# Attention and a gated feed-forward layer on one core: output tiles staged in reused load buffers, an exp and a mask emitted earlier, a weight fusion begun one step later

## The chip, the cores and the metric

One core of one Trainium2 chip. The metric is the device time of one execution in microseconds (us), lower is better. Executions of one kernel here spread by more than 1% to either side (the kernel before: 320.1 to 328.0 us in 34 runs of the first group, up to 330.1 us in another), so medians and many runs are used. With one core there is no second die to compare; a run counts as slow here only because it lies over 1.5% above the fastest of its kernel in the group. Two single executions lie far from all others and are unexplained: one of 1622 us among 35 runs of the kernel before (their median is 324.68 us with it and 324.50 without) and one of 1011 us in `only_buffers` (left out).

## The reference

```python
# attention: B=8, H=8, S=576, D=64, 16 extra "beacon" keys seen by every query
k_all  = concat([beacon_k, k]); v_all = concat([beacon_v, v])
scores = scale * q @ k_all.T           # causal on the 576 keys
a      = softmax(scores); x = a @ v_all  # -> 4608 tokens x 512
# feed-forward: d_model 512, d_ff 1024
h   = ((x @ w1) * (x @ w2)) @ w3
out = h @ w_out                        # 4608 x 512, float32
```

## The kernel before

The kernel fuses `w3 @ w_out` once into one 1024x512 matrix `Wt`, so the feed-forward layer is two products, a multiply and one more product. Attention runs in 64 steps (a pair of heads, half of the query tiles). Each step emits: the scores of the next step (TensorE), two exps of them (ScalarE), one or two masks (VectorE), the value matmuls of this step (TensorE), and between them "fill": a slice of the feed-forward matmuls of an earlier token chunk, drawn one at a time from a generator with `emit_ff(n)`. A fill group of four matmuls with `w1` (call it A) is copied by ScalarE to `a_sb`; a group of four with `w2` (B) is multiplied with it on VectorE. Output groups of eight matmuls are scaled by VectorE into an output tile and written out.

```python
early = ctx.enter_context(tc.tile_pool(name="early", bufs=8))   # float32 loads of the first two batches
asb = ctx.enter_context(tc.tile_pool(name="asb", bufs=2))
op = ctx.enter_context(tc.tile_pool(name="op", bufs=3))         # output tiles, 256 KB each
psS = ...bufs=2 (score banks)   psM = ...bufs=3 (everything else)
# ... (cut)
def ff_out(mc, gT):
    for mt in range(4):
        pm = psM.tile([P, 512], FP32, name="pm")
        # ... 8 matmuls, one per emit_ff unit
        ot = op.tile([P, DM], FP32, name="ot")
        nc.vector.tensor_scalar(ot, pm, float(1.0 / GS), None, ALU.mult)
        nc.sync.dma_start(out[ds(mc * 512 + mt * P, P), :], ot)
        yield
# ... (cut) the start: first batch, steps 0 to 7
for s in range(NSB):                      # NSB = 8 steps per batch
    if 0 < s < NSB - 2:
        ahead(s + 2)                      # scores and exps, two steps ahead
    if s < 4:
        spin(1)                           # one dummy matmul
    if s == 4:
        rows.append(w3_transposed(0))     # fusion of w3 with w_out begins
    emit_ff((0, 0, 0, 0, 4, 6, 6, 6)[s])
    values(s)
# ... (cut) the steady state
for s in range(NSB, NS):
    b, r = s // NSB, s % NSB
    if more:
        scores(s + 1)
        exps(s + 1, 0)
    values(s)
    # ... (cut)
    k1 = min(8 if b > 1 else 4, fill[s])
    emit_ff(k1)
    if more:
        exps(s + 1, 1)
        mask(s + 1, 0)
    emit_ff(fill[s] - k1)                 # fill[s] is about 8 to 12
    if more:
        mask(s + 1, 1)
```

Two things matter later. VectorE serves masks, products, outputs and the normalisation from one queue, in the order of emission. And `exps(s + 1, 1)` and `mask(s + 1, 0)` stand at the same place, so moving one moves the other.

The softmax here doesn't subtract the row's maximum and nothing guards it: scores larger than these inputs give would overflow.

Of the kernel before, what the change touches and what calls it, by code (L numbers as in the profile page):

```python
# [8 lines left out]
FP32 = mybir.dt.float32  # L9
# [30 lines left out]
def kernel(  # L40
# [14 lines left out]
    B, H, S, D = q.shape  # L55
    Nb = beacon_k.shape[2]
    P = 128
    NT = H // 2
    DM = H * D
# [5 lines left out]
    RUN = 6  # L65
# [24 lines left out]
    early = ctx.enter_context(tc.tile_pool(name="early", bufs=8))  # L90
    tiny = ctx.enter_context(tc.tile_pool(name="tiny", bufs=2))
    bkp = ctx.enter_context(tc.tile_pool(name="bkp", bufs=1))
    asb = ctx.enter_context(tc.tile_pool(name="asb", bufs=2))
    op = ctx.enter_context(tc.tile_pool(name="op", bufs=3))
    psS = ctx.enter_context(tc.tile_pool(name="psS", bufs=2, space=bass.MemoryType.PSUM))
    psV = ctx.enter_context(tc.tile_pool(name="psV", bufs=1, space=bass.MemoryType.PSUM))
    psM = ctx.enter_context(tc.tile_pool(name="psM", bufs=3, space=bass.MemoryType.PSUM))
# [24 lines left out]
    def load_v(b, jt):  # L122
        load_kv(b, jt, v, beacon_v, vas[b % NB2][:, jt, :, 0:64])
# [10 lines left out]
    def load_pair(b, t):  # L134
        for i, src in enumerate((q, k)):
            st = early.tile([P, 2, RUN * D], FP32, name="st")
            if b:
                nc.vector.memset(st[0:1, 0, 0:1], 0.0)
            nc.sync.dma_start(
                st[:NR], src[b, ds(2 * t, 2)].rearrange("h (p j) d -> p h (j d)", j=RUN)  # L140
            )
            early_qk[b, t, i] = st
        if t == 0:
            bst = bkp.tile([Nb, H, D], FP32, name="bst")
            nc.sync.dma_start(bst, beacon_k[b].rearrange("h n d -> n h d"))
            early_b[b] = bst
# [3 lines left out]
    def cast_pair(b, t):  # L150
        o16s[t] = []
        for i in range(2):
            o16 = tiny.tile([P, RUN, P], FP16, name=f"o16_{i}")
            nc.vector.tensor_copy(  # L154
                o16[:NR].rearrange("p j (h d) -> p h j d", h=2),
                early_qk[b, t, i][:NR].rearrange("p h (j d) -> p h j d", j=RUN),
            )
            o16s[t].append(o16)
        if t == 0:
            b16 = bkp.tile([Nb, DM], FP16, name="b16")  # L160
            nc.vector.tensor_copy(b16, early_b[b].rearrange("p h d -> p (h d)"))
            early_b[b] = b16
# [38 lines left out]
    def spin(n):  # L201
        pm = psM.tile([P, 512], FP32, name="pm")
        for _ in range(n):
            nc.tensor.matmul(pm, zeros[:, 0:P], zeros)
# [13 lines left out]
    for t in range(NT):  # L218
# [6 lines left out]
        fill=0.0,  # L225
# [3 lines left out]
    for m, base in (  # L229
# [10 lines left out]
            fill=0.0,  # L240
# [15 lines left out]
    def w3_transposed(kt):  # L256
        pt = psM.tile([P, NFT, P], FP16, name="pm")
        for rt in range(NFT):
            nc.tensor.transpose(pt[:, rt, :], w316[:, kt // 2, kt % 2, ts(rt, P)], ident)  # L259
        wT = wp.tile([P, NFT, P], FP16, name="wT")  # L260
        nc.vector.tensor_copy(wT, pt)  # L261
        return wT
# [45 lines left out]
# [3 lines that stand above are left out]
            for kf in range(NFT):  # L311
                nc.tensor.matmul(  # L312
                    pm,
                    gT[:, kf, ts(mt, P)],
                    Wt[:, kf, :],
                    start=(kf == 0),
                    stop=(kf == NFT - 1),
                )
                if kf < NFT - 1:
                    yield  # L320
            ot = op.tile([P, DM], FP32, name="ot")
            nc.vector.tensor_scalar(ot, pm, float(1.0 / GS), None, ALU.mult)  # L322
            nc.sync.dma_start(out[ds(mc * 512 + mt * P, P), :], ot)
            yield
# [11 lines left out]
    def emit_ff(n):  # L336
        nonlocal emitted
        for _ in range(n):
            try:
                next(ff)  # L340
            except StopIteration:
                return
            emitted += 1
# [4 lines left out]
    def scores(s):  # L348
        b, t, half = s // (2 * NT), (s // 2) % NT, s % 2
        if half == 0:  # L350
            pTs[s // 2] = ptp.tile([P, 2, PW], FP16, name="pT")
        qT, kT = qTs[b % NB2], kTs[b % NB2]
        pss[s] = []
        for g in (2 * half, 2 * half + 1):
            ps = psS.tile([P, 2, 512], FP32, name="ps")
            pss[s].append(ps)
            for jt, q0, n, col in GROUPS[g]:
                for hh in range(2):
                    nc.tensor.matmul(  # L359
                        ps[:, hh, ds(col, n)],  # L360
                        kT[ds(hh * 64, 64), t, ts(jt, P)],
                        qT[ds(hh * 64, 64), t, ds(q0, n)],
                    )

    def exps(s, j):
        g = 2 * (s % 2) + j
        pT = pTs[s // 2]
        nc.scalar.activation(  # L368
            pT[:, :, ds(GO[g], GW[g])], pss[s][j][:, :, 0 : GW[g]], AF.Exp, scale=scale
        )  # L370
# [13 lines left out]
    def values(s):  # L384
        b, t, half = s // (2 * NT), (s // 2) % NT, s % 2
        tiles = ([0, 1], [2, 3, 4])[half]
        pT = pTs[s // 2]
        va = vas[b % NB2]
        if t == 0 and half == 0:
            x16s[b] = xp.tile([P, NJT, DM], FP16, name="x16")  # L390
        x16 = x16s[b]
        ni = len(tiles)
        pv = psV.tile([P, 6, VS], FP32, name="pv")
        for n, i in enumerate(tiles):
            for hh in range(2):
                for jn, (jt, col) in enumerate(BLK[i]):
                    nc.tensor.matmul(  # L397
                        pv[:, 2 * n + hh, 0:65],
                        pT[:, hh, ds(col, P)],
                        va[:, jt, 2 * t + hh, 0:65],  # L400
                        start=(jn == 0),
                        stop=(jn == len(BLK[i]) - 1),
                    )
        rd = sm.tile([P, 6], FP32, name="rd")
        nc.vector.reciprocal(rd[:, 0 : 2 * ni], pv[:, 0 : 2 * ni, 64])  # L405
        nc.vector.tensor_tensor(  # L406
            x16[:, ds(tiles[0], ni), ds(t * P, P)].rearrange("p i (h d) -> p i h d", h=2),
            pv[:, 0 : 2 * ni, 0:64].rearrange("p (i h) d -> p i h d", h=2),
            rd[:, 0 : 2 * ni]
            .rearrange("p (i h) -> p i h", h=2)  # L410
            .unsqueeze(3)
            .to_broadcast([P, ni, 2, 64]),
            ALU.mult,
        )
        if t == NT - 1 and b > 1:
            for i in tiles:
                nc.sync.dma_start_transpose(  # L417
                    xT[:, :, ds(b * S + QT0[i], QTN[i])], x16[: QTN[i], i, :]
                )
# [5 lines left out]
    fill = [0] * NS  # L425
# [9 lines left out]
    def ahead(s):  # L435
        scores(s)
        for j in range(2):
            exps(s, j)

    def masks(s):  # L440
        for j in range(2):
            mask(s, j)
# [39 lines left out]
    for s in range(NSB):  # L482
        if 0 < s < NSB - 2:
            ahead(s + 2)
        if s < 4:
            spin(1)
        if s == 4:
            rows.append(w3_transposed(0))
        emit_ff((0, 0, 0, 0, 4, 6, 6, 6)[s])
        values(s)  # L490
        if 0 < s < NSB - 2:
            masks(s + 2)
        if s == 5:
            for t in range(NT):
                load_pair(1, t)
# [13 lines left out]
    for s in range(NSB, NS):  # L509
        b, r = s // NSB, s % NSB  # L510
        more = s + 1 < NS and s + 1 != 2 * NSB
# [4 lines that stand above are left out]
        if b == 1 and r % 2 == 0 and r < NSB - 2:  # L516
            pe_transpose_pair(1, r // 2 + 1)
            if r < NSB - 4:
                cast_pair(1, r // 2 + 2)
        k1 = min(8 if b > 1 else 4, fill[s])  # L520
        emit_ff(k1)
        if more:
            exps(s + 1, 1)
            mask(s + 1, 0)
        emit_ff(fill[s] - k1)
        if more:
            mask(s + 1, 1)
        if s == 2 * NSB - 1:
            pe_transpose_x(1)
            ahead(s + 1)  # L530
            emit_ff(8)
            masks(s + 1)
        if 1 <= b < B - 1:
            if r == 0:
                for c in range(NJT if b > 1 else 0):
                    load_v(b + 1, c)
                for c in range(NJT if b + 2 < B else 0):
                    load_q(b + 2, c)
                    load_k(b + 2, c)
            if 1 <= r <= NJT:  # L540
                transpose_qk(b + 1, r - 1)
# [31 lines left out]
```

## Time and profile before

| | before |
|---|---|
| median of 3 runs | 324.72 us (323.89 to 326.23) |
| the profiled run | 322.48 us, span 320.7 us, mean granted clock 0.989 |
| TensorE busy | 92% |
| VectorE, ScalarE, GpSimd busy | 52%, 49%, 34% |
| TensorE waits for masks after 60 us | 6.9 us in 6 waits |
| TensorE waits for exps after 60 us | 4.5 us in 16 waits |
| VectorE waits for output buffers after 60 us | 9.1 us in 3 waits |

The lines behind these rows stand in the prediction. One view that it doesn't show is the chain of work that ended last, as shares of the span by engine:

```profile
PE 69%; ACT 9%; DMA 9%; DVE 6%; SPq 3%; issue 2%; POOL 1%; DVEq 0%
```

So 69% of the path to the end is TensorE's own work, and 9% and 6% are ScalarE's and VectorE's: an exp, a copy or a mask on which the next step of the path waited. That 15% (48 us) is not all to be won: much of it lies at the start, and TensorE was idle for only 25.9 us of the whole span (320.7 - 294.8), since it did other work during many of these steps.

### The profile page before, as it was taken

The numbers are of one execution on the slowest core, as the hardware profiler recorded it, in microseconds if no ns is written. First come the engines' busy times: TensorE is split into PE (matmuls) and PEld (weight loads), VectorE is DVE, ScalarE is ACT, GpSimd is POOL, SyncE is SP. The second block draws the span as 40 slices with busy tenths as digits, with TensorE's granted clock in tenths as the row PEclk, the third lists the DMA queues.
The fourth block names the chain that finished last, engine by engine and source line by source line (L and its number), as shares of the span: only waits on it lengthen the run. The fifth ranks groups of instructions, "written<-read, shape, count | busy, mean of one in ns | idle before, by whom it ended". The sixth has DMA issues, their size and how long they took to land.

```text
span 320.7 us, 7011 instructions
## 1 busy us (share of the span) xinstructions
PE 294.8 (92%) x2822; PEld 151.9 (47%) x2822; DVE 167.0 (52%) x391; ACT 156.4 (49%) x230; POOL 109.5 (34%) x147
## 2 busy tenths in 40 slices
PE   7879898998999998999899969998999999999995
PEld 3446554545454454445444434444445444444442
DVE  5744455765465544554555455555555555343342
ACT  2972237675546645654565536644654662230320
POOL 8855727538970295029403850140000000000000
PEclk9897999999999999999999999999999999999999
DMA  7999999999999499949997999595424003402103
GB/s 200 197 207 197 224 259 150 142 145 155 175 211 158 79 132 226 160 73 185 192 150 70 132 216 134 100 164 151 77 53 139 33 3 63 143 0 88 45 0 131
DMA packets 156960, 42.97 MB, mean 134 GB/s; under 512 B 143104, under 2 KB 151296, under 8 KB 156928
## 3 DMA queue, kind: packets, MB, share of 16 engines
q0 software_dynamic: 102240, 17.28, 74.4%
q1 hardware_dynamic: 54688, 25.25, 41.0%
q8 instruction: 22, 0.36, 0.5%
q14 instruction: 10, 0.08, 0.1%
HBM read 39.32 MB, written 9.44 MB: 152 GB/s over the span
## 4 chain that ended last, share of the span: by engine, by line
PE 69%; ACT 9%; DMA 9%; DVE 6%; SPq 3%; issue 2%; POOL 1%; DVEq 0%
PE pm L291 32%; PE pm L312 14%; PE pv L397 9%; PE ps L359 7%; ACT pT L368 6%; DMA out_dram<-ot 5%; PE pm L269 4%; SPq L417 2%; DMA xT<-in_moe_w_dram 2%; ACT a_sb L302 2%; DVE ot L322 2%; DMA st<-in_k_dram 1%; PE pm L259 1%; DVE gT L304 1%; DVE pT L380 1%
## 5 line engine op out<-in xcount | busy, mean ns | idle before, releaser
L291 PE MATMUL pm<-xT,w 128*128 128x512 f16 x576 | 132.7, 379 | 2.0 <-DVE ot L322 1.1
L368 ACT ACTIVATE pT<-ps 128x736 f16<-128x736 f32 (+3 forms) x128 | 105.8, 866 | 36.0 <-PE ps L359 35.6
L302 ACT ACTIVATE a_sb<-pm 128x512 f32<-128x512 f32 x72 | 43.0, 598 | 96.1 <-PE pm L291 96.1
L291 PEld LDWEIGHTS <-w 128*128 128x128 f16 x576 | 53.6, 98 | 61.5 <-issue 3.2
L304 DVE TENSOR_TENSOR gT<-pm,a_sb 128x512 f16<-128x512 f32 x72 | 49.7, 691 | 47.8 <-PE pm L291 47.7
L312 PE MATMUL pm<-Wt,gT 128*128 128x512 f16 x288 | 65.6, 379 | 0.0
L113 POOL DMA_DIRECT2D va<-in_v_dram x40 | 35.0, 885 | 73.0 <-PE pv L397 64.9
L397 PE MATMUL pv<-va,pT 128*128 128x65 f16 x960 | 42.1, 196 | 7.7 <-DVE pT L380 7.6
L322 DVE TENSOR_SCALAR ot<-pm 128x512 f32<-128x512 f32 x36 | 24.9, 692 | 37.7 <-PE pm L312 24.0
L359 PE MATMUL ps<-qT,kT 64*128 64x80 f16 (+3 forms) x704 | 38.5, 231 | 6.0 <-ACT pT L368 5.6
L397 PEld LDWEIGHTS <-pT 128*128 128x128 f16 x960 | 34.5, 99 | 18.1 <-DVE pT L380 8.9
L312 PEld LDWEIGHTS <-gT 128*128 128x128 f16 x288 | 26.9, 98 | 30.0 <-issue 0.2
L359 PEld LDWEIGHTS <-kT 64*128 64x128 f16 x704 | 21.1, 96 | 35.0 <-issue 33.2
L405 DVE RECIPROCAL rd<-pv 128x4 f32<-128x4 f32 x64 | 12.1, 190 | 44.3 <-PE pv L397 44.3
L406 DVE TENSOR_TENSOR x<-pv,rd 128x256 f16<-128x256 f32 x64 | 31.4, 491 | 2.4
L113 POOL DMA_DIRECT2D k<-in_k_dram x30 | 26.0, 866 | 11.0 <-DMA w<-in_moe_w_dram 7.0
L104 POOL DMA_DIRECT2D q<-in_q_dram x30 | 26.2, 875 | 10.0 <-DMA w<-in_moe_w_dram 6.4
L380 DVE TENSOR_TENSOR pT<-pT,MB 128x512 f16<-128x512 f16 x64 | 19.9, 323 | 0.0
L269 PE MATMUL pm<-wo,wT 128*128 128x512 f16 x64 | 16.9, 395 | 1.0 <-DVE wT L261 1.0
L380 DVE TENSOR_TENSOR pT<-pT,MA 128x480 f16<-128x480 f16 x32 | 12.9, 403 | 2.1 <-ACT pT L368 1.9
L154 DVE CAST o<-st 96x768 f16<-96x768 f32 x16 | 9.3, 609 | 3.9 <-DMA st<-in_q_dram 2.2
L261 DVE COPY wT<-pm 128x1024 f16<-128x1024 f16 x8 | 5.5, 692 | 9.7 <-PE pm L259 9.7
(43 smaller groups left out, 95.8 us busy)
## 6 DMA issues: line engine op xcount, KB each, us to landing
out_dram<-ot SPq DMA_DIRECT2D x36, 256.0 KB, 4.4
va<-in_v_dram POOLq DMA_DIRECT2D x24, 128.0 KB, 6.9
q<-in_q_dram POOLq DMA_DIRECT2D x24, 128.0 KB, 8.1
st<-in_q_dram SPq DMA_DIRECT2D x8, 288.0 KB, 6.8
st<-in_k_dram SPq DMA_DIRECT2D x8, 288.0 KB, 7.8
k<-in_k_dram POOLq DMA_DIRECT2D x18, 128.0 KB, 8.0
xT<-in_moe_w_dram POOLq DMA_DIRECT2D x8, 256.0 KB, 9.8
w<-in_moe_w_dram POOLq DMA_DIRECT2D x8, 256.0 KB, 11.8
```

Of the source, the lines that this page charges most:

```text
L113: nc.gpsimd.dma_start(dst[ds(p0, rows)], src[b, :, ds(s0, rows), :].rearrange("h s d -> s h d"))
L269: nc.tensor.matmul(pm, wT[:, rt, :], wo16[:, rt, :], start=(rt == 0), stop=(rt == NFT - 1),)
L291: nc.tensor.matmul(pm, w12[:, kt, ds(i * DF + kf * P, P)], xT[:, kt, ds(mc * 512, 512)], start=(kt == 0), stop=(kt == NKT - 1),)
L302: nc.scalar.activation(a_sb, pm, AF.Copy, scale=GS)
L304: nc.vector.tensor_tensor(gT[:, kf, :], pm, a_sb, ALU.mult)
L312: nc.tensor.matmul(pm, gT[:, kf, ts(mt, P)], Wt[:, kf, :], start=(kf == 0), stop=(kf == NFT - 1),)
L322: nc.vector.tensor_scalar(ot, pm, float(1.0 / GS), None, ALU.mult)
L359: nc.tensor.matmul(ps[:, hh, ds(col, n)], kT[ds(hh * 64, 64), t, ts(jt, P)], qT[ds(hh * 64, 64), t, ds(q0, n)],)
L368: nc.scalar.activation(pT[:, :, ds(GO[g], GW[g])], pss[s][j][:, :, 0 : GW[g]], AF.Exp, scale=scale)
L380: nc.vector.tensor_tensor(blk, blk, m.unsqueeze(1).to_broadcast([P, 2, n]), ALU.mult)
L397: nc.tensor.matmul(pv[:, 2 * n + hh, 0:65], pT[:, hh, ds(col, P)], va[:, jt, 2 * t + hh, 0:65], start=(jn == 0), stop=(jn == len(BLK[i]) - 1),
L406: nc.vector.tensor_tensor(x16[:, ds(tiles[0], ni), ds(t * P, P)].rearrange("p i (h d) -> p i h d", h=2), pv[:, 0 : 2 * ni, 0:64].rearrange ...
```

## The change

The change takes the three output buffers away and stages outputs in the eight buffers that held the float32 loads of the first two batches (idle from about 61 us on). It emits the second exp of a step, with the first mask beside it, after 4 fill matmuls instead of 8 (from the third batch on; in the second batch it was 4 already). It begins the fusion at step 5 instead of 4, with one dummy matmul in its place, and the memory freed goes in part to a third `a_sb` buffer.

```diff
-    asb = ctx.enter_context(tc.tile_pool(name="asb", bufs=2))
-    op = ctx.enter_context(tc.tile_pool(name="op", bufs=3))
+    asb = ctx.enter_context(tc.tile_pool(name="asb", bufs=3))
@@ ff_out
-            ot = op.tile([P, DM], FP32, name="ot")
+            ot = early.tile([P, 2, RUN * D], FP32, name="st")
+            ot = ot.rearrange("p h r -> p (h r)")[:, 0:DM]
@@ start
-        if s < 4:
+        if s < 5:
             spin(1)
-        if s == 4:
+        if s == 5:
             rows.append(w3_transposed(0))
-        emit_ff((0, 0, 0, 0, 4, 6, 6, 6)[s])
+        emit_ff((0, 0, 0, 0, 0, 4, 6, 6)[s])
@@ steady state
-        k1 = min(8 if b > 1 else 4, fill[s])
+        k1 = min(4, fill[s])
         emit_ff(k1)
```

Simply adding a fourth buffer to the output pool is not open to this kernel: built that way, 6.25 KB per partition were left for a pool of 8 KB, and it didn't fit. That build never ran.

## The prediction

> **What bounds the kernel now.** I read the page first, then the waits of TensorE after 60 us, the waits of VectorE in the same stretch, then the timeline around each long wait.
>
> ```profile
> span 320.7 us, 7011 instructions
> PE 294.8 (92%) x2822; PEld 151.9 (47%) x2822; DVE 167.0 (52%) x391; ACT 156.4 (49%) x230; POOL 109.5 (34%) x147
> ```
>
> TensorE is the bound: 92% busy, every other engine near half. No arithmetic leaves the kernel, so a gain can only come out of TensorE's idle time and its slow-clock time.
>
> ```profile
> PE pv L397 <- DVE pT L380: 6.9, 6, 2.8
> PE ps L359 <- ACT pT L368: 4.5, 16, 0.3
> PE pm L291 <- DVE ot L322: 1.1, 1, 1.1
> ...
> DVE ot L322 <- DMA out_dram<-ot: 9.1, 3, 4.0
> DVE ot L322 <- PE ps L359: 4.5, 2, 2.3
> ```
>
> Columns: us in total, times, longest. TensorE waits for masks (L380) a few times but long, for exps (L368) often but short. VectorE in turn waits 9.1 us for output buffers (L322) to be written out. The "ps" row with 4.5 us has the same cause, I think: its two waits (152.23 and 217.15 us) end 0.1 us after an output write landed (152.14, 217.05). The longest case:
>
> ```profile
> 178.21 8.39 SPq L323 DMA_DIRECT2D out_dram<-ot  x4
> ...
> 185.55 0.69 DVE L322 TENSOR_SCALAR ot<-pm 128x512 f32<-128x512 f32 x1 [3.97 <-DMA out_dram<-ot]
> ...
> 186.16 0.40 DVE L380 TENSOR_TENSOR pT<-pT,MA 128x480 f16<-128x480 f16 x1
> 186.61 0.35 PE L397 MATMUL pv<-va,pT 128*128 128x65 f16 x6 [2.82 <-DVE pT L380]
> ```
>
> The fourth output tile of a token chunk finds all three buffers in flight; the first write, issued at 178.21, lands at 185.45. VectorE stands 3.97 us, the mask behind it is late, TensorE stands 2.82 us. The short waits repeat every 7.7 us:
>
> ```profile
> 235.73 0.60 ACT L302 ACTIVATE a_sb<-pm 128x512 f32<-128x512 f32 x1 [1.17 <-PE pm L291]
> 236.22 2.42 ACT L368 ACTIVATE pT<-ps 128x800 f16<-128x800 f32 x3
> 236.49 0.33 PE L359 MATMUL ps<-qT,kT 64*128 64x128 f16 x4
> ...
> 237.10 0.40 PE L359 MATMUL ps<-qT,kT 64*128 64x256 f16 x4 [0.28 <-ACT pT L368]
> 237.27 0.23 DVE L380 TENSOR_TENSOR pT<-pT,MB 128x160 f16<-128x160 f16 x1
> 237.43 0.90 PE L397 MATMUL pv<-va,pT 128*128 128x65 f16 x24
> ```
>
> The second exp of a step (800 wide) stands in program order behind an a_sb copy that needs 8 fill matmuls; the next scores need the score bank that this exp empties. At the start:
>
> ```profile
> 23.01 0.62 PE L259 MATMUL pm<-ident,xT 128*128 128x128 f16 x8 [1.31 <-DMA xT<-in_moe_w_dram]
> 24.41 1.89 PE L269 MATMUL pm<-wo,wT 128*128 128x512 f16 x4 [0.79 <-DVE wT L261]
> ```
>
> The fusion of w3 with w_out waits for w3, then for a copy, and then four matmuls take 1.89 us where later four take 1.03: the clock has dropped.
>
> **What the Trainium skill says.** "TensorE: Matmul & The Clock Gate", Part 1, "Architectural detail": ScalarE and VectorE queues are strict FIFO. The case at 185 us agrees: mask and a_sb copies wait behind an instruction they don't depend on. The same page, "What's actually happening": the clock is halved after a little-used window of 3413 ns. The trace agrees: its clock record is 0.5 from 14.2 to 17.6 and from 24.4 to 27.9 us, one such window each. "DMA: Bandwidth & Descriptors", "Issuing engines are not separate DMA queues": transfers from all queues run on the same 16 engines and interleave. The trace agrees: output writes land 2.0 us after issue when alone (292 us on) and after up to 7.9 us beside the loads. "Perfetto Trace Analysis", "Optimization Strategy": the same gap repeating on the engine that should be full can mean that buffers ran out. The 0.28 us gaps are that, with a score bank freed late.
>
> **The change part by part.**
>
> *Output buffers, 3 to 8.* No instruction is added; the tensor_scalar keeps its 0.69 us, the write its 256 KB. The early buffers are last read at about 61 us (the last cast begins at 60.4) and the first output is at 81.6, so nothing old is waited for. At most four outputs come per chunk, and chunks are some 30 us apart until 275 us, against 7.9 us for the slowest landing: with eight buffers this wait should be zero. TensorE's idle time behind it in the timeline: 1.15 (at 122.7), 1.13 (153.3), 2.82 (186.6), 1.10 (218.2), and some 0.36 hidden in the stream at 277 (22 matmuls at 0.2165 us should show 4.76 and their tail, they show 5.15). Sum 6.56 us, all on the path, since TensorE has no other work in its queue that may pass. Rounded: 6.5.
>
> *Second exp after 4 fill matmuls instead of 8.* In steps whose fill is "B A B" (A = four matmuls copied by ScalarE, B = four multiplied by VectorE), the exp now comes before A's copy: it runs directly after the first exp, about 234.55 to 235.4 in the case shown, and the bank is free 1.1 us before it is wanted. In "A B A" steps ScalarE's order stays the same, and on VectorE a 0.41 us mask moves ahead of a product into idle time. What one occurrence costs: start of scores to first fill matmul after the 24 value matmuls is 1.68 us in the waiting steps (139.95 to 141.63) and 1.23 in a step without (93.00 to 94.23), so 0.45, of which 0.28 shows as idle. Not all comes back: the last ten value matmuls need the second mask, which still follows the second B product. That mask ends 1.01 us after the scores start (140.96), plus 0.06 to be seen; without the exp wait the ten would begin at 0.49 + 14 x 0.035 = 0.98. So 0.09 is taken over by the mask, leaving 0.36. There are 14 such rows (125.2 to 259.8): 14 x 0.36 = 5.0 us.
>
> *Fusion one step later, a spin in its place.* The 64 fusion matmuls and 64 transposes stay; 0.22 us of spin is added. Gone: the 1.31 us wait for w3 (lands at 22.96; now wanted about 23.6). New: the scores of step 7 follow at once and wait for the exps of step 6 (ScalarE is through them at 23.2), about 0.9 us with smaller ones. The 0.79 for the copy stays. The later waits (0.19, 0.58, 0.38) change to about as much, as my step-by-step list has 3.1 us of stalls against 3.3. So 0 by waits. What is left is the clock: the half-speed window costs 3.4 / 2 = 1.7 us. [...]I give 0.55 to keeping the clock: +0.9 us.
>
> *A third a_sb buffer.* No wait on one is in the trace (all 96.1 us before a_sb are for matmuls): 0.
>
> Sum 6.5 + 5.0 + 0.9 = 12.4 us. I take off 1 us for new waits (below): 11.4, so 324.7 - 11.4 = 313.3 us.
>
> **The rivals.**
>
> *Transfers become the bound.* Output writes share SyncE's queue with the transposes that feed the next block. For: the last two transposes for a block land at 171.44, its first scores are at 171.6. Against: the first scores need only the first four query pieces (168.6) and two key pieces; and those transposes stand behind the fourth output, so they move forward with it. The tightest is the xT piece landing at 118.56 for matmuls at 118.96; between cause and use lies no wait that the change removes. At worst 0.3 to 0.8 us per block in four blocks: total 315 to 316.
>
> *The wait behind the exp is only exchanged for the mask.* If the mask comes 0.2 us later than I count, the second part gives 2 us, not 5: 316.
>
> *Output waits are not TensorE's loss*, because other delays lie behind them: then only the exp part shows, about 319, inside 2%. Against: TensorE shows no second releaser in those gaps.
>
> *Start gets worse*, with a second slow window: +2 us, 315.
>
> **Range and chances.** Both large parts are read off idle time of the bounding engine, so half of the sum (6.3 us, about 2%) should come even where I am wrong on one. The runs before spread 323.9 to 326.2, and the profiled one, 322.5, is the best of them, so that the output waits in other runs may be larger than these. Range 309.8 to 317.4. Faster by over 2% means under 318.2: 0.90; within 2%: 0.09; slower: 0.01.
>
> **What would show it.** Right: no wait of the output scaling for its write (9.1 now); TensorE's waits for masks from 6.9 to about 2 after 60 us; its waits for exps from 4.5 to under 1, with some 0.1 us waits for masks in place; period of two steps 7.7 to 7.35 us; no wait for w3; one slow window instead of two. Wrong: new waits of scores or L291 for transposes, more waits of TensorE for masks, or a second slow window at 25 to 40 us.

## The result, and the profile after

| | before | after |
|---|---|---|
| median of 4 runs each, side by side | 324.34 us (323.89 to 326.23) | 310.88 us (310.23 to 312.13) |
| ratio after / before, 95% interval | | 0.958 (0.953 to 0.963): faster |
| span of the profiled run | 320.7 us | 309.7 us |
| TensorE busy | 92% | 96% |

Ratios here and below are the mean time of one kernel's fast runs over that of the other's of the same rounds, so they are not quite the ratio of the medians that I quote.

The page after, its head and its chain:

```profile
span 309.7 us, 7001 instructions
PE 295.8 (96%) x2823; PEld 153.4 (50%) x2823; DVE 168.1 (54%) x391; ACT 158.1 (51%) x230; POOL 108.9 (35%) x147
...
PE 79%; DMA 8%; DVE 4%; ACT 3%; SPq 2%; issue 2%; POOL 1%; DVEq 0%
```

TensorE's busy time is what it was (294.8 before, 295.8 now); the span is 11.0 us shorter, so the gain is idle time. In the chain ScalarE falls from 9% to 3%.

TensorE's waits after 60 us (total, times, longest), first of the changed kernel, then those of VectorE:

```profile
PE pv L397 <- DVE pT L380: 1.9, 3, 0.7
...
PE ps L359 <- ACT pT L368: 0.2, 1, 0.2
PE ps L359 <- DMA qT<-q: 0.2, 1, 0.2
```

```profile
DVE st L322 <- PE pm L311: 24.8, 33, 2.0
```

Masks: 6.9 to 1.9 us. Exps: 4.5 to 0.2. VectorE's output row for its own writes (9.1 us) is gone, and so is the row of 4.5 us that the prediction put down to the same cause: the only thing that an output still waits for is its matmuls. One small wait for a transfer (0.2 us for a transposed query piece) stands in no row of the first profile; the repeat of the kernel before has one too (0.5 us).

The place of the longest wait before, a token chunk's fourth output, in the timeline of the changed kernel:

```profile
176.80 0.40 DVE L380 TENSOR_TENSOR pT<-pT,MA 128x480 f16<-128x480 f16 x1
...
177.82 0.69 DVE L322 TENSOR_SCALAR st<-pm 128x512 f32<-128x512 f32 x1 [0.62 <-PE pm L311]
...
179.03 0.36 PE L397 MATMUL pv<-va,pT 128*128 128x65 f16 x6
```

The mask now comes ahead of the fourth output, the output waits for its matmuls alone, and the six value matmuls have no wait in brackets (2.82 us before). Note that both parts of the change are visible here at once: the buffer is free, and the mask has moved ahead of the output. Which of them did it cannot be read from this trace.

The steady state, two steps at the end of the same block:

```profile
223.76 1.53 ACT L368 ACTIVATE pT<-ps 128x768 f16<-128x768 f32 x2
...
225.74 0.60 ACT L301 ACTIVATE a_sb<-pm 128x512 f32<-128x512 f32 x1 [0.44 <-PE pm L290]
...
226.50 0.55 PE L359 MATMUL ps<-qT,kT 64*128 64x128 f16 x8
...
226.98 1.07 PE L397 MATMUL pv<-va,pT 128*128 128x65 f16 x24
227.28 0.23 DVE L380 TENSOR_TENSOR pT<-pT,MB 128x160 f16<-128x160 f16 x1
```

The two exps run back to back at 223.76, ahead of the copy, and the eight scores at 226.50 run as one group without a wait. But the 24 value matmuls now show 1.07 us instead of 0.90: the second mask ends at 227.51, inside them. A pair of such steps takes 7.4 us, not the 7.7 of before (219.09 to 226.50 from scores to scores).

The start:

```profile
24.51 0.62 PE L258 MATMUL pm<-ident,xT 128*128 128x128 f16 x8
25.92 1.89 PE L268 MATMUL pm<-wo,wT 128*128 128x512 f16 x4 [0.79 <-DVE wT L260]
```

The wait for w3 (1.31 us) is gone, but the first four fusion matmuls still take 1.89 us, the mark of half speed. The clock record has 10.2 us at half speed at the start, three windows, where before had two (6.8 us) and the prediction expected one. The first scores of step 8 start at 49.55 us, against 49.20 before. That looks as if the third part gave nothing, but this execution was late before the part could act: the dummy matmul of step 3, up to which the two programs do the same, started at 21.05 us and at 20.09 before. From there to the scores of step 8 it took 28.50 us, against 29.11 before, 0.6 us less.

### The profile page after: what moved, and what is told of

The parts are those of the page before. It is cut to its first block, busy times and chain, and to the rows that moved or that the text cites. A ratio compares the mean times of both kernels' runs of the same rounds, so it can differ in the third digit from the quotient of the medians.

```text
span 309.7 us, 7001 instructions
## 1 busy us (share of the span) xinstructions
PE 295.8 (96%) x2823; PEld 153.4 (50%) x2823; DVE 168.1 (54%) x391; ACT 158.1 (51%) x230; POOL 108.9 (35%) x147
## 4 chain that ended last, share of the span: by engine, by line
PE 79%; DMA 8%; DVE 4%; ACT 3%; SPq 2%; issue 2%; POOL 1%; DVEq 0%
PE pm L290 34%; PE pm L311 18%; PE pv L397 11%; PE ps L359 8%; PE pm L268 5%; DMA qT<-q 3%; DMA k<-in_beacon_k_dram 2%; DMA st<-in_k_dram 2%; ACT pT L368 2%; PE pm L258 1%; SPq L128 1%; DVE gT L303 1%; POOL va L112 1%; SPq L138 1%; DVE o L153 1%
## 5 line engine op out<-in xcount | busy, mean ns | idle before, releaser
L112 POOL DMA_DIRECT2D va<-in_v_dram x40 | 34.2, 872 | 66.4 <-PE pv L397 57.4
L397 PE MATMUL pv<-va,pT 128*128 128x65 f16 x960 | 44.4, 196 | 2.6 <-DVE pT L380 2.5
L397 PEld LDWEIGHTS <-pT 128*128 128x128 f16 x960 | 35.6, 99 | 13.6 <-issue 6.5
L311 PEld LDWEIGHTS <-gT 128*128 128x128 f16 x288 | 26.9, 98 | 30.0 <-issue 0.2
L359 PE MATMUL ps<-qT,kT 64*128 64x80 f16 (+3 forms) x704 | 36.3, 232 | 2.5 <-ACT pT L368 1.9
L322 DVE TENSOR_SCALAR st<-pm 128x512 f32<-128x512 f32 x36 | 24.9, 691 | 25.0 <-PE pm L311 24.8
L103 POOL DMA_DIRECT2D q<-in_q_dram x30 | 26.7, 890 | 10.2 <-DMA va<-in_v_dram 6.3
L153 DVE CAST o<-st 96x768 f16<-96x768 f32 x16 | 10.2, 666 | 4.1 <-DMA st<-in_q_dram 2.8
L279 ACT CAST Wt<-pm 128x512 f16<-128x512 f32 x8 | 4.7, 585 | 14.9 <-PE pm L268 14.9
```

Of the source, the lines that this page charges most:

```text
L103: nc.gpsimd.dma_start(q16s[b % NB2][:rows, c, :].rearrange("s (h d) -> s h d", h=H), q[b, :, ds(c * P, rows), :].rearrange("h s d -> s h d"),)
L112: nc.gpsimd.dma_start(dst[ds(p0, rows)], src[b, :, ds(s0, rows), :].rearrange("h s d -> s h d"))
L311: nc.tensor.matmul(pm, gT[:, kf, ts(mt, P)], Wt[:, kf, :], start=(kf == 0), stop=(kf == NFT - 1),)
L359: nc.tensor.matmul(ps[:, hh, ds(col, n)], kT[ds(hh * 64, 64), t, ts(jt, P)], qT[ds(hh * 64, 64), t, ds(q0, n)],)
L397: nc.tensor.matmul(pv[:, 2 * n + hh, 0:65], pT[:, hh, ds(col, P)], va[:, jt, 2 * t + hh, 0:65], start=(jn == 0), stop=(jn == len(BLK[i]) - 1),
```

## The experiments

The theory going in: the time came from TensorE's idle time behind (1) outputs waiting for a buffer and (2) the second exp, with the start giving little. The rivals: the order of masks behind the waiting output is what matters, not the buffer; the exp part is only an exchange for mask waits; the start gives more, by the clock; and other changes of the bundle (the third `a_sb`) matter. Runs of one group shared a chip and the runs of the kernel before.

| run | median us (runs) | kernel before beside it | ratio (95%) |
|---|---|---|---|
| before_again | 324.48 (14) | 324.68 (35) | 1.005 (1.001 to 1.009) |
| only_buffers | 316.95 (5) | 324.68 | 0.977 (0.972 to 0.982) |
| only_exp | 316.10 (6) | 324.68 | 0.976 (0.970 to 0.982) |
| only_fusion | 322.58 (22) | 324.68 | 0.994 (0.991 to 0.997) |
| two_outputs | 344.84 (6) | 325.78 (11) | 1.057 (1.051 to 1.064) |
| last_output_early | 317.10 (6) | 325.78 | 0.972 (0.966 to 0.978) |
| mask_without_exp | 319.74 (6) | 325.78 | 0.980 (0.974 to 0.986) |
| exp_without_mask | 321.54 (6) | 325.78 | 0.985 (0.979 to 0.991) |
| after_again | 310.14 (5) | 324.46 (11) | 0.957 (0.954 to 0.960) |
| after_mask_sooner | 308.72 (6) | 324.46 | 0.951 (0.948 to 0.954) |
| after_old_fusion | 312.38 (6) | 324.46 | 0.963 (0.960 to 0.967) |
| after_two_asb | 310.61 (6) | 324.46 | 0.957 (0.953 to 0.960) |

All twelve gave correct results. At a threshold of 2% the verdict on `only_buffers`, `only_exp`, `mask_without_exp` and `exp_without_mask` is unclear, since their intervals hold 0.98, but all lie well below 1.

Of the eleven reference runs of the second group (the four rows against 325.78) four are labelled slow. The ratios of these rows come out only with the mean of all eleven (326.16 us), so slow runs are in them. The seven fast ones have a median of 324.79 us; I take the gains of this group from that, so that the gains are 1.0 us smaller than the table suggests and the loss of `two_outputs` 1.0 us larger. With the means of fast runs the ratio of `last_output_early` would be 0.976 and not 0.972.

**before_again**: the kernel before, unchanged, as a control.

> The kernel before against itself: ratio 1.000, within 0.3%. My theory that the output waits vary from run to run and explain why most runs before take about 2 us more than the profiled one (322.5): then the page of this run shows VectorE waiting for output writes by another sum than 9.1 + 4.5 us, and a longer run has a larger sum. The rival, that the half-speed clock windows at the start make the difference: then the mean clocks of the runs differ and the slower runs have the lower clock.

It came out at 1.005, though it is the same program, and the interval leaves out 1. One run of the reference set took 320.07 us, and 14 of the others, being more than 1.5% above that, were labelled slow; that this is what shifts the ratio is likely and not shown. The medians, over all runs, agree within 0.2 us, and in the other three rows of this group ratio and medians agree within 0.3%. I use the medians for this group.

The theory, that output waits vary between runs, isn't borne out. VectorE's row in its profile:

```profile
DVE ot L322 <- DMA out_dram<-ot: 14.0, 5, 3.8
```

That seems to be more than the 9.1 us in 3 waits of the first profile, but there two more waits (4.5 us) are put down to "PE ps". The five waits stand at the same five places in both timelines (at 122, 152, 186, 217 and 276 us in the first, within 1.2 us of that in the repeat): 13.6 and 14.0 us. The rival has some support: over the 34 runs time falls as the granted clock rises, by about 1.4 us per 0.01 (correlation -0.64).

**only_buffers**: the buffers alone.

```diff
-    op = ctx.enter_context(tc.tile_pool(name="op", bufs=3))
-            ot = op.tile([P, DM], FP32, name="ot")
+            ot = early.tile([P, 2, RUN * D], FP32, name="st")
+            ot = ot.rearrange("p h r -> p (h r)")[:, 0:DM]
```

> The output buffers alone (8 early ones instead of 3; exp, fusion and the a_sb count as before). My theory: 6.5 us less, up to 8.5 if the unprofiled runs before wait longer for their writes: 316 to 318, ratio 0.974 to 0.980; no wait of the scaling for its write; TensorE's long waits for masks at 153, 187 and 218 us gone; the 0.28 us waits for exps still there, 14 or so. Rival (other delays lie behind): under 3 us.

Measured: 324.68 to 316.95, 7.7 us. TensorE's waits:

```profile
PE ps L359 <- ACT pT L368: 4.5, 16, 0.3
PE pv L397 <- DVE pT L380: 1.8, 3, 0.7
```

VectorE's output waits are gone, mask waits fall to 1.8 us, and the 16 exp waits of 4.5 us stay as they were. The first term of the prediction (6.5) is confirmed in kind and a little larger.

**only_exp**: the earlier exp and mask alone, three output buffers kept.

```diff
-        k1 = min(8 if b > 1 else 4, fill[s])
+        k1 = min(4, fill[s])
```

> The second exp after 4 fill matmuls alone. In the trace of the changed kernel a pair of steps takes 7.40 us instead of 7.70, 14 pairs: 4.2 us, and 0.4 near 97 us. My theory: 4 to 5 us less, 319 to 320.5, ratio 0.985 to 0.988, waits for output writes as before. Rival: that the two parts only work together, since a stalled VectorE eats what the earlier exp gains: under 2 us.

Measured: 324.68 to 316.10, 8.6 us, where the prediction had 5.0 for this part. Its timeline around a fourth output shows why:

```profile
179.58 0.40 DVE L380 TENSOR_TENSOR pT<-pT,MA 128x480 f16<-128x480 f16 x1
...
181.81 0.35 PE L397 MATMUL pv<-va,pT 128*128 128x65 f16 x6
...
183.89 0.69 DVE L322 TENSOR_SCALAR ot<-pm 128x512 f32<-128x512 f32 x1 [3.91 <-DMA out_dram<-ot]
...
184.63 1.89 PE L291 MATMUL pm<-xT,w 128*128 128x512 f16 x8 [1.60 <-DVE ot L322]
```

VectorE still stands 3.91 us for a buffer. But the mask is through at 179.98, ahead of that wait, so the value matmuls run at 181.81 without one, and four more fill matmuls run before TensorE stops, for 1.60 us and not 2.82. So this part also takes about half of the output wait away from TensorE, without touching the wait itself: TensorE's rows for masks and for output buffers together were 6.9 + 1.1 = 8.0 us before, are 1.9 + 2.8 = 4.7 here, and 1.8 with the eight buffers. I had not seen this, and the 8.6 us lie outside what I expected of the run.

**only_fusion**: the later fusion alone (the diff's third part).

> The later start of the fusion alone. In the two profiled runs the scores of step 8 start at 49.20 before and at 49.55 us after, with 3.4 us more of half-speed clock in the latter: I expect 0 +- 1 us (ratio 0.997 to 1.003), no wait for w3, and the score start of step 8 to move with the number of half-speed windows. Rival (the prediction's): a slow window saved in most runs, 1 to 2 us faster.

Measured over 22 runs: 324.68 to 322.58, 2.1 us, outside the 0 ± 1 us that I expected; the mean granted clock is 0.992 against 0.986 (0.988 in the reference runs labelled fast). In its profiled run step 8 began at 47.05 us without any half-speed window at the start, against 49.20 (two windows) and 48.80 in the two profiles of the kernel before. This profile also holds the clearest case of what a long stand costs. Columns: the stretch, its length, busy time (and instructions) of TensorE, weight loads, VectorE, ScalarE and GpSimd, the granted clock, DMA share, GB/s:

```profile
180.00:184.00 4.00, 2.29 (x23) 1.02 (x21) 0.08 (x1) 1.30 (x2) 1.99 (x4) 1.00 1.31 178
184.00:188.00 4.00, 2.70 (x12) 1.22 (x13) 1.99 (x5) 0.00 (x0) 2.95 (x4) 0.55 2.14 194
188.00:192.00 4.00, 4.00 (x31) 1.64 (x30) 1.49 (x4) 1.93 (x3) 0.90 (x2) 0.60 1.92 192
```

TensorE stood 3.01 us for a late mask, until 185.30 us; the clock record then is at half from 184.4 to 191.2 us. In the first profile the same place stood 2.82 us and kept its clock.

**two_outputs**: the wait made worse on purpose.

```diff
-    op = ctx.enter_context(tc.tile_pool(name="op", bufs=3))
+    op = ctx.enter_context(tc.tile_pool(name="op", bufs=2))
```

> The kernel before with two output buffers instead of three: the suspected cost doubled. Theory (VectorE stands behind a write, TensorE behind VectorE, and long stands cost the clock as well): the third output waits too, some 3 us after its own ready time in four chunks, and the fourth still; 8 to 14 us slower, 332 to 339, mean clock lower. Rival (the waits are elsewhere hidden): within 2%, under 331.

Measured: 324.79 (fast runs) to 344.84, 20.0 us slower, well beyond the 8 to 14 us expected; mean clock 0.958 against 0.983 in the fast runs. TensorE's waits, then VectorE's:

```profile
PE pv L397 <- DVE pT L380: 21.0, 8, 6.5
```

```profile
DVE ot L322 <- DMA out_dram<-ot: 30.0, 8, 7.3
```

VectorE's wait grew by 16.4 us over the 13.6 us of the first profile, TensorE's wait for masks by 14.1, and three half-speed stretches (23.9 us in all) began during TensorE's three longest stands. The rival that output waits are not TensorE's loss falls.

**last_output_early**: only the fourth output of a chunk gets an early buffer; the first three keep the pool of three.

```diff
-            ot = op.tile([P, DM], FP32, name="ot")
+            if mt < 3:
+                ot = op.tile([P, DM], FP32, name="ot")
+            else:
+                ot = early.tile([P, 2, RUN * D], FP32, name="st")
+                ot = ot.rearrange("p h r -> p (h r)")[:, 0:DM]
```

> The kernel before, with every fourth output tile alone in an early buffer, the other three in their own pool: four places in flight instead of three, no place for a fifth. If only the fourth output of a chunk lacks a buffer (my reading), this equals the eight buffers: 316 to 317.5, no wait of the scaling for its write. If more than four are in flight at times, a wait remains and it lies between 317.5 and 324.

Measured: 324.79 (fast runs) to 317.10, 7.7 us, as much as all eight buffers (7.7). No wait for an output buffer is left. One free buffer more than three is the whole of the first part.

**mask_without_exp** and **exp_without_mask** split what `only_exp` moved together (the edits in outline).

```diff
# mask_without_exp                     # exp_without_mask
+        emit_ff(min(4, fill[s]))      +        emit_ff(min(4, fill[s]))
+        mask(s + 1, 0)                +        exps(s + 1, 1)
+        emit_ff(up to 8 in all)       +        emit_ff(up to 8 in all)
+        exps(s + 1, 1)                +        mask(s + 1, 0)
         emit_ff(the rest)                      emit_ff(the rest)
```

> The kernel before, with only the first mask of the next step emitted after 4 fill matmuls; the second exp stays after 8, three output buffers. Theory A (the two parts of the change overlap: in the steps where the fourth output waits, the mask now stands ahead of it in VectorE's queue, so TensorE isn't held up for the values): TensorE's waits for masks after 60 us fall from about 7 to 2 us though VectorE still waits 12 us or so for output writes; 3 to 4.5 us faster, 320 to 321.5. Theory B (the earlier exp alone gave all of the 8.6 us that exp and mask gave together): no change, 324 to 325.

> The kernel before, with only the second exp after 4 fill matmuls; the mask stays after 8, three output buffers. Theory A: 14 x 0.30 = 4.2 us and 0.4 near 97 us, so 4 to 5 us faster, 319.5 to 320.7, two steps in 7.40 us, and TensorE's waits for masks still about 7 us after 60 us. Theory B: 8 to 9 us, 316.

Measured, from 324.79 (fast runs): the mask alone 319.74, 5.1 us; the exp alone 321.54, 3.3 us, a little under the 4 to 5 expected. The profile of the exp alone holds a 3.4 us half-speed window after a stand of 3.02 us. The waits of TensorE and VectorE with the mask alone:

```profile
PE ps L359 <- ACT pT L368: 4.5, 16, 0.3
PE pm L291 <- DVE ot L322: 2.3, 3, 1.2
PE pv L397 <- DVE pT L380: 1.8, 3, 0.6
```

```profile
DVE ot L322 <- DMA out_dram<-ot: 13.2, 5, 3.2
```

and with the exp alone:

```profile
PE pv L397 <- DVE pT L380: 7.8, 6, 3.0
...
PE ps L359 <- ACT pT L368: 0.2, 1, 0.2
```

With the mask alone the exp waits stay (4.5) and the mask waits fall to 1.8, although VectorE still waits 13.2 us for buffers. With the exp alone it is the reverse. So the two act on different waits, and the mask's place cures part of what the buffers cure: TensorE's rows for masks and output buffers go from 8.0 us to 1.8 + 2.3 = 4.1, where the buffers leave 1.8.

**after_again, after_old_fusion, after_two_asb**: the changed kernel, and it with one part taken back (the old fusion start; `asb` with 2 buffers).

> The changed kernel again, as the yardstick for the next three on the same chip: 310 to 312 us, ratio to before 0.955 to 0.962. Its clock record should show slow windows only in the first 30 us and the last 3.

> The changed kernel with the fusion begun at step 4 as before. Alone on the kernel before, the later fusion gave 2.1 us in the medians of 22 runs. If the start adds independently of the rest: 1.5 to 2.5 us slower than after_again, 313. Rival (the start's gain is a matter of clock windows that the other parts already keep): no difference.

> The changed kernel with two a_sb buffers instead of three. No wait on such a buffer is in either trace: within 0.2% of after_again. Rival (with VectorE's products later behind the masks, the third buffer is what lets ScalarE run ahead): 1 us or more slower, and waits of a_sb for the product in the trace.

Measured: 310.14, 312.38 and 310.61 us. The gain is confirmed (324.46 to 310.14, 14.3 us, 0.957). Taking the later fusion back costs 2.2 us, as much as it gave alone, so it adds to the rest. The third `a_sb` buffer is worth nothing that 6 runs could show. One thing in the profile of `after_two_asb` is hardly in the others (0.2 us at most after 60 us): TensorE waited 3.0 us (2 waits, near 64 and 68 us) for a load of `w`.

**after_mask_sooner**: the second mask, to which the exp's wait was partly exchanged, four fill matmuls after the first.

```diff
-        emit_ff(fill[s] - k1)
+        k2 = min(4, fill[s] - k1)
+        emit_ff(k2)
         if more:
             mask(s + 1, 1)
+        emit_ff(fill[s] - k1 - k2)
```

> The changed kernel with the second mask of the next step emitted after 8 fill matmuls instead of after all 12, so that it no longer stands behind the last product on VectorE. In the trace of the changed kernel the 24 value matmuls of a pair take 0.91 us to the first fill matmul, against 0.74 where nothing is waited for: 0.17 us in 14 pairs or more. My theory (the wait behind the exp was handed to this mask): two steps in 7.25 us instead of 7.40, 2 to 2.5 us faster than after_again, 308.5. Rival (that gap is something else, the products or the value bank): no difference.

Measured: 308.72 us, against 310.14 of the changed kernel in the same group: 1.4 us by the medians, 2.0 by the means, where 2 to 2.5 were expected. All six runs (306.97 to 309.46) lie below all five of the changed kernel (309.86 to 311.19), so this version beats both kernels. Its timeline:

```profile
215.32 0.56 DVE L380 TENSOR_TENSOR pT<-pT,MB 128x512 f16<-128x512 f16 x2
...
216.26 0.55 PE L359 MATMUL ps<-qT,kT 64*128 64x128 f16 x8
...
216.75 0.90 PE L397 MATMUL pv<-va,pT 128*128 128x65 f16 x24
```

Both masks now run together before the scores, and the 24 value matmuls are back at 0.90 us. A pair of steps takes 7.23 us (209.03 to 216.26), 0.17 less than 7.4.

## Why the prediction was right or wrong

The forecast, 313.3 us in 309.8 to 317.4, held: 310.88. The gain was 13.5 us where 11.4 was forecast. Of the difference 1.0 us was taken off for new waits that hardly came; the parts measured alone (7.7, 3.3 without the mask, 2.1) differ from their forecasts (6.5, 5.0, 0.9) by +1.2, -1.7 and +1.2 us. Each of these is uncertain by about 1 us, and the errors have both signs, so that the sum came so close is in part luck. The steps:

- **Output buffers, 6.5 us: right, at most a little small.** From scores to scores, the four steps with a long wait took 4.63, 4.53, 6.21 and 4.50 us and now take 3.33 or 3.34, together 6.5 us, so the sum read off the timeline was right for the run it was read from. Over many runs the part gives 7.7. The prediction thought that other runs might have larger output waits; the repeat shows 14.0 us against 13.6, so that isn't it. A stand near 3 us can cost the clock as well. By the mean clocks (0.990 with the buffers, 0.986 to 0.988 without) and the slope above the clock would be 0.3 to 0.6 us of it; that is an estimate from these numbers, and the rest is no more than the spread.
- **The second exp, 5.0 us: right in mechanism, one term mis-sized.** The exp waits went from 4.5 to 0.2 us, as said. The term that was off is "So 0.09 is taken over by the mask": it measured 0.17. Value matmuls to first fill took 0.74 us and take 0.91 now (219.57 to 220.48). So a pair of steps gained 0.30 us, not 0.36 (7.7 to 7.4, where 7.35 was forecast), and 14 x 0.30 = 4.2 us. The exp alone shows the same 7.4 us (195.05 to 202.45 in its profile) and gave 3.3. after_mask_sooner confirms it from the other side: with that mask earlier the 0.17 goes away. The rival "only exchanged for the mask" was true for 0.17 of the 0.45 us.
- **What the prediction missed: the mask that moves with the exp.** It counted the moved mask as going "into idle time". In fact it moves ahead of the output that waits, and TensorE no longer stands for that wait in full: 5.1 us alone. This didn't spoil the sum, because with free buffers there is little left for it to save: mask waits are 1.8 us with the buffers alone and 1.9 in the changed kernel (no run has the buffers and the exp without the mask). It does mean that the parts are not additive: alone they give 7.7 + 8.6 + 2.1 = 18.4 us, together 13.5 to 14.3. Counting the exp without its mask, 7.7 + 3.3 + 2.1 = 13.1 us, the sum closes within 1.2 us. The rows of TensorE's waits after 60 us say the same: in all 13.6 us before, 7.4 with the buffers (6.2 less), 6.3 with exp and mask (7.3 less), but 3.4 with all (10.2 less).
- **The start, 0.9 us: too small, and the step "So 0 by waits" failed.** It gave 2.1 us alone and 2.2 in the bundle. The prediction's list had 3.1 us of stands against 3.3, so no gain, and put all of it on the clock. In the nine profiles with the early fusion TensorE waits 1.1 to 2.6 us for w3, in the five with the late one 0 to 0.4 us, and the new stands are small. All gaps between matmuls, from the dummy matmul of step 3 to the scores of step 8, come to 3.0 to 4.5 us with the early start (mean 3.8) and 2.0 to 2.4 us with the late one (mean 2.1). So waits make up a large part of the gain: this stretch takes 29.4 us on average with the early start and 27.4 with the late one. The clock has a share: half-speed time in the stretch was 3.0 us on average against 0.7. But it isn't needed for a gain: of the profiles without any half-speed time there, the two early ones take 28.5 and 27.7 us and the four late ones 26.9 to 27.3.
- **The clock.** A sentence that weighed the chance of keeping the clock by how full a window is with matmuls has been cut from the prediction, because the traces don't bear it out. Counted as it counted, without transposes, the window before the first drop was about a third full, and not the 22% it gave. Over the runs, a window of some 40% was followed by half speed (the changed kernel, 22.5 to 25.9 us) and one of some 30% was not (`mask_without_exp`, 23.1 to 26.5 us). With transposes TensorE was busy for 2.55 of the 3.40 us before the first drop. So "little-used" in the prediction's passage on the clock is not shown here; the length of the window (3.4 us) is. What decides whether a window is lost at the start stays open.
- **A smaller misreading.** The prediction says of the case at 185 us that "mask and a_sb copies" wait behind an instruction they don't depend on. That holds for the mask; the a_sb copy there (188.73 us) waited 4.05 us for its own matmuls.
- **The third `a_sb`, 0: right** (310.61 without it, 310.14 with it).
- **Transfers becoming the bound: right that it is small.** Waits for transposed query pieces are 0.2 to 0.6 us in four of the five profiles of the changed kernel and its variants, and absent in the fifth, which has the 3.0 us for `w` instead; the medians show no loss from it.
- **The bound:** TensorE's busy time stayed (294.8 and 295.8 us), and the gain was idle time and clock, as the first paragraph of the prediction said.

## What to carry to other kernels

When an engine that works in order may wait for a buffer, look at what stands behind that instruction in its queue: one more buffer cured the wait here (7.7 us), emitting the urgent work first cured more than half of what it cost TensorE (5.1 us), and the gains don't add. Where two changes act on the same wait, measure each alone and both together before giving either its share. And read a stand of the main engine as its length plus the clock that it may lose, over several runs, since one profile can show none of it. Before two profiles are compared at one place, look whether they were level at the last point up to which both programs do the same.

## What the Trainium skill lacked or had wrong

- "TensorE: Matmul & The Clock Gate", "Why this matters for your kernels", warns of gaps over about 3 us. The runs agree: between 60 and 300 us, the five stands of 3.01 to 6.53 us in the fourteen profiles each go with 3.4 to 10.2 us at half clock, and none of the shorter ones (up to 2.82 us) does. The page lacks how much later half-speed windows vary between executions: between 11 and 32 us they took 0 to 10.2 us from profile to profile (6.8 and 10.2 us in two profiles of the changed kernel). It also has no case of an output buffer missing on another engine that costs TensorE's clock (mean clock 0.958 with two output buffers, 0.983 with three, fast runs).
- "Perfetto Trace Analysis", "Optimization Strategy", says that consistent bubbles can mean too few buffers, and the gaps of 0.28 us here were of that kind. The section lacks that the gap shown can be less than the loss: 0.28 us showed as idle per pair of steps, and curing it and the mask wait that took its place gave 7.70 - 7.23 = 0.47 us.
- No page that I read says what a strictly ordered queue means for the order in which work is emitted: one mask moved ahead of an output that waits for a buffer was worth 5.1 us, though VectorE's wait itself stayed (13.2 us).
